# Storing one head's two gradients in pieces of 76, 48 and 4 rows from SyncE, and the last head's in halves: an attention-decode backward kernel on Trainium2

## The chip, the cores and the metric

The kernel runs on one core of one Trainium2 chip. The metric is device time in microseconds (us), as the median of several executions. Before the change it was 1286.64 us in three runs (1284.98 to 1289.45).

## The reference, cut to what matters

One query row per head attends to 8192 keys; wanted are the output and the gradients of q, k and v.

```python
B, H, Sq, Sk, D = 2, 32, 1, 8192, 128            # 64 heads, bf16

def _fwd_reference(q, k, v):
    scale = q.shape[-1] ** -0.5
    scores = jnp.einsum("bhqd,bhkd->bhqk", q, k) * scale
    p = _softmax(scores, axis=-1)
    return jnp.einsum("bhqk,bhkd->bhqd", p, v)

def reference(q, k, v, grad_out):
    _out, _vjp = jax.vjp(lambda *a: _fwd_reference(*a), q, k, v)   # shortened
    return (_out, *_vjp(grad_out))
```

For every head, k and v (2 MB each) are read and dk and dv (2 MB each) are written. dk and dv are outer products, so the arithmetic is small: 268.47 MB come in and 268.47 MB go out, and the memory traffic sets the time: 417 GB/s over the span before, with the DMA engines at nine tenths or more in 39 of the page's 40 slices.

## The kernel before

A head's k or v is one tile of 128 partitions with 64 rows of 128 numbers each. One partition of a 2 MB tile holds 16 KB. The gradient is written over the tile that held k or v, and stored from there; the load of a head six places later waits until that store has landed (116 such waits of SyncE's loads before, 1138.0 us in all).

```python
def by_rows(eng, dst, src, rows):                # a store cut along the partitions
    p = 0
    for m in rows:
        pin(eng.dma_start(out=dst[p : p + m], in_=src[p : p + m], max_dma_last_dim=NT * D))
        p += m

def outer(i, w, c, ends):                        # w = 1: v first, w = 0: k
    ...                                          # VectorE writes chunk c of the gradient
    if c + 1 in ends:
        at = ends.index(c + 1)
        b0, b1 = (ends[at - 1] if at else 0) * CH, (c + 1) * CH
        dst = (dv_v if w else dk_v)[i]
        if w == 0 and i in SPREAD:               # 7 of the 64 k stores: 126 + 2 rows
            by_rows(store_eng, dst, h.tile[w], (P - 2, 2))
        else:
            eng = load_eng if len(ends) > 1 else store_eng
            pin(eng.dma_start(out=dst[:, b0:b1, :], in_=h.tile[w][:, b0:b1, :]))

whole = [NCH]                                    # NCH = 4 chunks: one store
last = list(range(1, NCH + 1))                   # the last head: four quarters
...
for g in range(...):
    ...
    if x := within(O1):
        outer(x[0], 1, x[1], last if x[0] == BH - 1 else whole)
    if x := within(O0):
        outer(x[0], 0, x[1], last if x[0] == BH - 1 else whole)
```

`load_eng` is SyncE (queue q1 in the profile), `store_eng` is GpSimd (queue q0). So loads go through q1 and whole stores through q0, until the last head, 63, whose eight quarters go through q1. Both queues are served by the same 16 DMA engines: of their time the page gives q1 49.8% and q0 48.7%, and instructions (q8) 0.7%. After the loop, two small stores (o and dq, 16 KB each) leave from SyncE.

Of the kernel before, what the change touches and what calls it, by code (L numbers as in the profile page):

```python
# [20 lines left out]
SPREAD = range(5, 64, 9)  # L21
# [3 lines left out]
def kernel(  # L25
# [16 lines left out]
    BH = B * H  # L42
# [3 lines left out]
    NCH = NT // CH  # L46
# [3 lines left out]
    load_eng = nc.sync  # L50
# [32 lines left out]
    def by_rows(eng, dst, src, rows):  # L83
# [5 lines that stand above are left out]
# [299 lines left out]
    def outer(i, w, c, ends):  # L388

        h = heads[i]  # L390
        n0 = c * CH
        shape = [P, CH, D // 2, 2]
        pin(
            nc.vector.tensor_tensor(  # L394
                out=h.tile[w][:, n0 : n0 + CH, :].rearrange("p n (e t) -> p n e t", t=2),
                in0=h.qb[w][:]
                .rearrange("p (e t) -> p e t", t=2)
                .unsqueeze(1)
                .to_broadcast(shape),
                in1=h.pair[w][:, n0 : n0 + CH, :].unsqueeze(2).to_broadcast(shape),  # L400
                op=ALU.mult,
            )
        )
        if c + 1 in ends:
            at = ends.index(c + 1)
            b0, b1 = (ends[at - 1] if at else 0) * CH, (c + 1) * CH
            dst = (dv_v if w else dk_v)[i]
            if w == 0 and i in SPREAD:
                by_rows(store_eng, dst, h.tile[w], (P - 2, 2))
            else:  # L410
                eng = load_eng if len(ends) > 1 else store_eng
                pin(eng.dma_start(out=dst[:, b0:b1, :], in_=h.tile[w][:, b0:b1, :]))  # L412
# [3 lines left out]
    A0 = A1 + NCH  # L416
    O0 = A0 + 1
    whole = [NCH]
    last = list(range(1, NCH + 1))
    AHEAD = NTILE // 2  # L420

    prev = None
    for g in range(SL * BH + O0 + NCH + 4 - SL):
# [15 lines left out]
# [4 lines that stand above are left out]
        ev = None  # L443
        if g < SL * BH:
            i, r = divmod(g, SL)
# [74 lines left out]
```

## Time and profile before

| what | before |
|---|---|
| median of 3 runs | 1286.64 us |
| span of the profiled run, mean granted clock | 1286.9 us, 0.956 |
| traffic over the span | 417 GB/s |
| q1: loads, and head 63's stores | 272.70 MB, 49.8% of 16 engines |
| q0: whole stores | 264.25 MB, 48.7% of 16 engines |
| q8: instructions, 150 packets | 2.46 MB |

The page's list of DMA issues gives what, from which engine's queue, how often, KB each, and the median us from issue to landing. Two of its lines for the kernel before:

```profile
out_dram<-kvt POOLq DMA_DIRECT2D x119, 2048.0 KB, 66.9
out_dram<-kvt SPq DMA_DIRECT2D x8, 512.0 KB, 24.0
```

A whole store takes 67 us to land although its 8 rows per engine are only some 5 us of packets (8 x 0.61): it must stand in line behind other stores, which leave about every 10 us. At the end of the program such a line remains on each engine, and it isn't equally long on all of them: by the prediction's chains of packets the engines end their data between 1259.8 and 1284.7 us. The prediction below shows the lines of the end.

### The profile page before, as it was taken

To read this page: it belongs to the slowest core of one execution; us is meant where nothing else is said; L and a number is where in the kernel's file an instruction comes from. 1 tells how busy PE (TensorE), PEld (TensorE's weight loads), DVE (VectorE), ACT (ScalarE), POOL (GpSimd) and SP (SyncE) were. 2 spreads that over 40 slices of the span, in tenths; PEclk is the share of its full clock that TensorE was granted. 3 is DMA by queue.
4 is the path that set the end of the run, shared out by engine and by line. 5 is a ranking of instruction groups with operands and counts; after the bars stand their busy time and mean duration, and the time that the engine had idled before them with its cause. 6 is when DMAs were issued, how large, how long until landed. Compare 5 with 4: busy or idle time off the path is not lost.

```text
span 1286.9 us, 42575 instructions
## 1 busy us (share of the span) xinstructions
PE 1131.8 (88%) x19268; PEld 860.1 (67%) x19268; DVE 935.9 (73%) x2122; ACT 975.2 (76%) x641; POOL 75.1 (6%) x142
## 2 busy tenths in 40 slices
PE   6999999988899988989899988889898988988880
PEld 5777777766677666766666766667666666766650
DVE  2888888777687777767776876777767777777781
ACT  6888888877788777867777877778777777777750
POOL 0000000000000000000000000000000000000000
PEclk9999999999899999989899998999999999999985
DMA  9999999999999999999999999999999999999995
GB/s 388 424 425 427 427 427 427 426 427 428 428 426 427 428 427 426 416 429 427 427 427 429 427 427 427 427 424 424 426 427 428 426 427 424 427 428 428 424 392 216
DMA packets 39986, 539.68 MB, mean 419 GB/s; under 512 B 5116, under 2 KB 5116, under 8 KB 6396
## 3 DMA queue, kind: packets, MB, share of 16 engines
q1 hardware_dynamic: 20172, 272.70, 49.8%
q0 software_dynamic: 19632, 264.25, 48.7%
q8 instruction: 150, 2.46, 0.7%
q14 instruction: 32, 0.26, 0.0%
HBM read 268.47 MB, written 268.47 MB: 417 GB/s over the span
## 4 chain that ended last, share of the span: by engine, by line
DMA 38%; PE 26%; another core or an unknown queue 19%; DVE 10%; issue 4%; ACT 1%; SPq 1%; POOL 0%; POOLq 0%; DVEq 0%; ACTq 0%
DMA kvt<-in_v_dram 29%; PE tp L184 11%; PE acc L339 6%; DVE kvt L394 6%; DMA kvt<-in_k_dram 5%; DMA out_dram<-kvt 4%; PE dpw L195 3%; PE sw L195 3%; DVE sel L362 2%; ACT ev L186 1%; PE dpw L282 1%; SPq L98 1%; DVE sel L356 1%; DMA qd_nat<-in_q_dram 1%
## 5 line engine op out<-in xcount | busy, mean ns | idle before, releaser
L186 ACT COPY ev<-tp 128x2048 bf16<-128x2048 bf16 x512 | 954.4, 1865 | 266.1 <-PE tp L184 254.4
L184 PE MATMUL tp<-ident_bf,kvt 128*128 128x128 bf16 x8192 | 559.9, 223 | 91.6 <-DMA kvt<-in_v_dram 71.6
L394 DVE TENSOR_TENSOR kvt<-qb,pair 128x2048 bf16<-128x2048 bf16 x512 | 621.4, 1214 | 0.3
L184 PEld LDWEIGHTS <-kvt 128*128 128x128 bf16 x8192 | 490.5, 101 | 98.3 <-DMA kvt<-in_v_dram 75.1
L195 PEld LDWEIGHTS <-ev 128*128 128x128 bf16 x8192 | 243.1, 96 | 210.0 <-issue 152.5
L339 PE MATMUL acc<-kvt,dS_pad 128*64 128x512 bf16 x1024 | 169.2, 413 | 0.8 <-DVE dqT L379 0.8
L339 PE MATMUL acc<-kvt,E_pad 128*64 128x512 bf16 x1024 | 161.0, 395 | 0.0
L195 PE MATMUL dpw<-qdT,ev 128*128 128x1 bf16 x4096 | 140.8, 164 | 17.7 <-DVE qb L177 16.9
L362 DVE SCALAR_TENSOR_TENSOR sel<-acc,diag,sel 128x128 f32<-128x128 f32 x384 | 134.7, 351 | 13.6
L195 PE MATMUL sw<-qdT,ev 128*128 128x1 bf16 x4096 | 142.0, 164 | 1.2 <-ACT ev L186 1.2
L412 POOL DMA_DIRECT2D out_dram<-kvt x119 | 63.7, 536 | 1087.6 <-DVE kvt L394 922.1
L207 DVE TENSOR_REDUCE mp<-sw 128x1 f32<-128x64 f32 x64 | 14.4, 224 | 151.8 <-PE sw L195 151.8
L339 PEld LDWEIGHTS <-dS_pad 128*64 128x64 bf16 x1024 | 37.7, 111 | 24.7 <-issue 5.9
L247 DVE CAST E_pad<-E_f 128x64 bf16<-128x64 f32 x64 | 12.5, 195 | 55.4 <-ACT E_f L238 55.4
L339 PEld LDWEIGHTS <-E_pad 128*64 128x64 bf16 x1024 | 36.5, 109 | 21.4 <-issue 0.9
L376 PE MATMUL acc<-ones,sel 128*128 128x1 f32 x256 | 43.6, 239 | 6.2 <-DVE sel L362 6.2
L282 PE MATMUL dpw<-ld,ones 128*128 128x1 f32 x256 | 46.3, 250 | 0.1
L253 DVE CUSTOM_DVE_ANT_0 junk<-E_f,dpw 128x64 bf16<-128x64 f32 x64 | 14.1, 221 | 43.7 <-PE dpw L195 43.7
L376 PEld LDWEIGHTS acc<-ones,sel 128*128 128x128 f32 x256 | 39.3, 194 | 7.3 <-DVE sel L362 7.3
L356 DVE TENSOR_SCALAR sel<-acc,diag 128x128 f32<-128x128 f32 x128 | 44.1, 344 | 0.0
L177 DVE CAST qb<-dpw 128x128 bf16<-128x128 f32 x128 | 35.5, 277 | 6.2 <-PE dpw L168 6.2
L282 PEld LDWEIGHTS dpw<-ld,ones 128*128 128x128 f32 x256 | 38.2, 189 | 0.5 <-DVE ld L253 0.5
(44 smaller groups left out, 313.2 us busy)
## 6 DMA issues: line engine op xcount, KB each, us to landing
out_dram<-kvt POOLq DMA_DIRECT2D x119, 2048.0 KB, 66.9
kvt<-in_v_dram SPq DMA_DIRECT2D x64, 2048.0 KB, 20.9
kvt<-in_k_dram SPq DMA_DIRECT2D x63, 2048.0 KB, 20.9
out_dram<-kvt POOLq DMA_DIRECT2D x7, 2016.0 KB, 70.3
out_dram<-kvt SPq DMA_DIRECT2D x8, 512.0 KB, 24.0
kvt<-in_k_dram SPq DMA_DIRECT2D x2, 512.0 KB, 4.7
kvt<-in_k_dram SPq DMA_DIRECT2D x1, 1024.0 KB, 7.3
out_dram<-kvt POOLq DMA_DIRECT2D x7, 32.0 KB, 69.7
```

The source lines that it names most:

```text
L177: pin(nc.vector.tensor_copy(out=h.qb[w][:], in_=h.qbp))
L184: pin(nc.tensor.transpose(tp[:, t, :], src[:, c * CH + t, :], ident_bf[:]))
L186: pin(nc.scalar.copy(out=ev[:], in_=tp[:]))
L195: nc.tensor.matmul(dst[:, c * CH + t : c * CH + t + 1], lhsT=ev[:, t, :], rhs=qdT[:, w, i : i + 1], start=True, stop=True,)
L207: pin(nc.vector.reduce_max(out=h.mp[:], in_=h.s, axis=AX.X))
L282: nc.tensor.matmul(out, lhsT=ones[:].to_broadcast([P, P]), rhs=col, start=True, stop=True)
L339: nc.tensor.matmul(h.acc[w][g : g + CW, :], lhsT=wts[:, n0 : n0 + CW], rhs=rows[:, n0 : n0 + QT, :].rearrange("p n d -> p (n d)"), start=( ...
L356: nc.vector.tensor_scalar(out=h.sel[:], in0=block, scalar1=diag[:, 0:1], scalar2=None, op0=ALU.mult)
L362: nc.vector.scalar_tensor_tensor(out=h.sel[:], in0=block, scalar=diag[:, b : b + 1], in1=h.sel[:], op0=ALU.mult, op1=ALU.add,)
L376: nc.tensor.matmul(h.acc[w][:, 0:1], lhsT=h.sel[:], rhs=ones[:], start=True, stop=True)
L394: nc.vector.tensor_tensor(out=h.tile[w][:, n0 : n0 + CH, :].rearrange("p n (e t) -> p n e t", t=2), in0=h.qb[w][:] .rearrange("p (e t) -> ...
L412: pin(eng.dma_start(out=dst[:, b0:b1, :], in_=h.tile[w][:, b0:b1, :]))
```

## The change

The intent is to balance the 16 DMA engines at the end. Head 62's two stores are taken from GpSimd's queue and cut so that four engines carry 23 of the 128 rows each and the other twelve 3 each. The four are called engines 0 to 3 here. SyncE gets six larger pieces, so head 63's eight quarters become four halves.

```diff
-            if w == 0 and i in SPREAD:
+            if i == BH - 2:
+                by_rows(load_eng, dst, h.tile[w], (76, 48, 4))
+            elif w == 0 and i in SPREAD:
                 by_rows(store_eng, dst, h.tile[w], (P - 2, 2))
...
-    last = list(range(1, NCH + 1))
+    last = [NCH // 2, NCH]
```

## The prediction

> **What bounds the kernel now.** I began with the busy slices of the page, because the change touches only stores of the last two heads.
>
> ```profile
> PE   6999999988899988989899988889898988988880
> DMA  9999999999999999999999999999999999999995
> GB/s 388 424 425 427 427 427 427 426 427 428 428 426 427 428 427 426 416 429 427 427 427 429 427 427 427 427 424 424 426 427 428 426 427 424 427 428 428 424 392 216
> ```
>
> Each digit is a fortieth of the span (32 us). DMA is at 9 everywhere but in the last slice, where the rate halves to 216 GB/s: the body is bound by data movement, and the only loose time is the end. So I asked for stretches of the end (columns: us, busy us and instructions of PE, PEld, DVE, ACT, POOL, the granted clock, DMA share, GB/s).
>
> ```profile
> 1180.00:1230.00 50.00, 43.08 (x755) 32.79 (x752) 36.04 (x84) 37.45 (x27) 3.55 (x6) 1.00 1.01 424
> ...
> 1240.00:1246.00 6.00, 4.70 (x56) 2.75 (x56) 5.34 (x14) 1.86 (x1) 0.53 (x1) 0.84 0.86 339
> 1246.00:1258.00 12.00, 6.03 (x27) 2.44 (x23) 11.43 (x20) 0.00 (x0) 0.00 (x0) 0.50 1.01 420
> 1258.00:1262.00 4.00, 0.63 (x3) 0.36 (x3) 0.57 (x3) 0.00 (x0) 0.00 (x0) 0.50 0.84 349
> 1262.00:1274.00 12.00, 0.00 (x0) 0.00 (x0) 0.00 (x0) 0.00 (x0) 0.00 (x0) 0.50 0.57 241
> 1274.00:1281.00 7.00, 0.00 (x0) 0.00 (x0) 0.00 (x0) 0.00 (x0) 0.00 (x0) 0.50 0.41 169
> 1281.00:1287.00 6.00, 0.00 (x0) 0.00 (x0) 0.00 (x0) 0.00 (x0) 0.00 (x0) 0.50 0.05 19
> ```
>
> From 1262 us on nothing computes, yet stores run for 23 us more with a DMA share of 0.57, then 0.41: some of the 16 DMA engines have run dry while others still have a queue. The end is the end of the slowest single DMA engine, and the mean of the share says nothing of it.
>
> The timeline of the two issuing queues gives the arrivals:
>
> ```profile
> 1233.65 0.53 POOL L412 DMA_DIRECT2D out_dram<-kvt  x1 [8.19 <-DVE kvt L394]
> 1243.38 0.53 POOL L412 DMA_DIRECT2D out_dram<-kvt  x1 [9.19 <-DVE ld L253]
> ```
>
> ```profile
> 1245.80 11.98 SPq L412 DMA_DIRECT2D out_dram<-kvt  x8
> 1259.23 4.90 SPq L489 DMA_DIRECT2D out_dram<-nat  x2
> ```
>
> The first two are the stores of head 62 (v, then k), the third the eight quarters of head 63.
>
> No view splits packets by DMA engine, so I did it from the trace's packet records. An engine runs one packet at a time, and its next packet starts 3 to 4 ns before the recorded end of the one before; chaining back from the end, with every engine held to its known share of each SyncE store, gives 16 chains. Last data packet of each:
> - seven late chains: 1279.9, 1280.0, 1280.2, 1280.9, 1280.9, 1281.5 and 1284.7 us;
> - two at 1272.8 and 1273.7 us;
> - seven early: 1259.8 (three), 1260.2, 1260.7, 1261.3 and 1263.7 us.
>
> The span ends 2.05 us after the last packet of all (1284.85, then 1286.9). Why are there two groups? The 150 instruction-fetch packets (q8, 16 KB, about 1 us each) fall in a strict round of eight chains, some 19 us of work on each. The seven late ones are seven of these; the eighth is one of the two chains that the 126+2-row stores relieve (14 packets of 8 KB there instead of 126).
>
> [...] SyncE's queue holds 2258 completion packets, 141 x 16 and 2, and the 2 are the 58-row load's. [...] that load and the 6-row load at the start give a set of six chains [...], and only one of the eight instruction-fetch chains is among them, a relieved one. That places engines 0 to 3 in the early group. [...] in the trace a late engine alternates one by one (16 KB of q0, 4 KB of q1)[...].
>
> **The change part by part.** A 16 KB row costs 0.607 us from start to start (0.611 recorded, 4 ns overlap); the two 8 KB halves of a split row cost 2 x 0.305.
> 1. Before, each store of head 62 puts 8 rows on every engine. After, engines 0 to 3 get 19 + 3 + 1 = 23, the others 3.
> 2. Late engines: 2 stores x 5 rows fewer = 10 x 0.607 = **-6.1 us**. They have no idle time in the end stage, so they finish that much earlier: 1284.85 becomes 1278.8, the other six about 1274 to 1275.5.
> 3. Engines 0 to 3: 2 x 15 = 30 rows more, 18.2 us. Part of it fills holes: early chains idle 2.3 to 5.1 us around 1240 to 1245, waiting for head 62's k. Counting work from 1228 us: the five earliest candidates have 26 to 35 packets of 16 KB on q0 left (16 of them head 62) and 16 equivalents of head 63. After: 26 - 16 + 16 + 46 = 72, to 35 - 16 + 16 + 46 = 81, times 0.607 = 44 to 49 us: done at **1272 to 1277 us**. If the 1263.7 chain (39 packets) is one of them, 1280.
> 4. Head 63 in halves: the same bytes, 32 packets of 8 KB for 64 of 4 KB on each engine: 9.76 against 9.92 us, -0.16 us. The first half starts when the second quarter did (1247.8 instead of 1245.8); an early engine may idle, a late one has its backlog.
> 5. GpSimd issues two stores less (0.53 us each), off the path.
>
> Sum: the last packet at 1278.7 instead of 1284.85, about **6 us** less. Nothing before 1233 us is touched.
>
> **The rivals.**
> - *Engines 0 to 3 become the bound.* If the numbering were otherwise and they were late ones, 1281 + 18.2 + 2 = 1301 us (+1.1%). Against it: the set of six above, and that the change aims at them. In a milder form, an early engine with more backlog ends at 1280 and eats 1 to 2 us of the gain.
> - *A wait for a semaphore.* SyncE's issues rotate over eight completion semaphores, so issue n waits for n-8 to land. After the change the third half of head 63 waits for the 76-row piece of v. On engines 0 to 3 this is 38 packets of 8 KB, alternating with some 13 of 16 KB: 13 x 0.916 + 25 x 0.305 = 19.5 us after about 1234.5, so 1254, just when the half is ready (1253.9). The last small store waits for the 76-row piece of k: about 1268. Neither is the end, unless landings come 10 us later than this; then up to 1290.
> - *SyncE stalls on deep queues.* 2 x 46 packets can be queued on engines 0 to 3. Before, SyncE had up to 72 (8 stores of 8 packets and a completion) queued on a late engine without stopping; its issues took 0.8 to 1.7 us instead of 0.34. A stall of a few us is hidden behind the late engines' backlog; a long one would cost up to 8 us, 1289.
> - *Hidden anyway*, about 1286: against it, nothing but stores runs in the last 23 us.
>
> **Range and chances.** 1286.64 - 6 = 1280.6; I take 1281.0 as engines 0 to 3 may be the last in some runs. The three runs of before spread over 4.5 us, and the late chains lie within 5 us of each other, so 1277.5 to 1285.5. A gain over 2% would need 26 us, more than the whole idle tail holds: 1%. A loss over 2% needs the wrong engines and a stall: 1%.
>
> **What would show it.** In the profile after: SyncE issues six stores of head 62 at about 1234 and 1243; the DMA share stays near 1 until 1258 without the dip to 0.86 at 1240, and is well above 0.57 between 1262 and 1274; by engine, four chains with 92 packets of 8 KB for head 62 where the others have 12, ending at 1272 to 1280, and the late ones 6 us earlier. The prediction is wrong if one of those four chains ends last by more than 2 us, if SyncE stands in an issue or a wait for head 62's landings past 1265, or if the late chains do not move by 6 us.

## The result, and the profile after

| | before | after |
|---|---|---|
| median of the rounds together (4 runs each) | 1288.05 us | 1307.70 us |
| lowest to highest | 1284.98 to 1296.05 | 1305.86 to 1308.69 |
| span, clock of the profiled run | 1286.9 us, 0.956 | 1306.9 us, 0.952 |

The ratio is 1.0141, with a 95% interval from 1.0093 to 1.0190: slower by some 18 us, where 6 us less were predicted. A ratio here is the mean time of one kernel's fast runs over that of the other's of the same rounds, so it isn't quite the ratio of the medians. The loss is under 2%, but far outside the range of 1277.5 to 1285.5.

The page's busy slices of the kernel after (tenths of DMA busy time, and the rate, in fortieths of the span):

```profile
DMA  9999999999999999999999999999999999999982
GB/s 387 425 427 429 425 427 427 428 427 426 428 427 428 427 429 415 425 428 427 428 426 423 426 426 428 427 426 425 426 428 430 426 424 425 429 427 427 403 283 95
```

Up to slice 37 nothing has moved. The last two slices fell from 392 and 216 GB/s to 283 and 95: all the loss lies in the end, where the change is. The stretches of the end, with the columns of the prediction (us, busy us of PE, PEld, DVE, ACT, POOL, granted clock, DMA share, GB/s), of the kernel after:

```profile
1240.00:1246.00 6.00, 5.17 (x84) 3.54 (x82) 4.61 (x14) 3.52 (x4) 0.00 (x0) 1.00 0.84 289
1246.00:1258.00 12.00, 7.07 (x29) 3.04 (x29) 11.78 (x20) 0.00 (x0) 0.00 (x0) 0.50 0.81 277
1258.00:1262.00 4.00, 0.90 (x3) 0.63 (x3) 2.25 (x8) 0.00 (x0) 0.00 (x0) 0.50 0.81 240
1262.00:1274.00 12.00, 0.00 (x0) 0.00 (x0) 0.00 (x0) 0.00 (x0) 0.00 (x0) 0.50 0.91 304
1274.00:1281.00 7.00, 0.00 (x0) 0.00 (x0) 0.00 (x0) 0.00 (x0) 0.00 (x0) 0.50 0.72 225
1281.00:1287.00 6.00, 0.00 (x0) 0.00 (x0) 0.00 (x0) 0.00 (x0) 0.00 (x0) 0.50 0.28 94
1287.00:1307.00 20.00, 0.00 (x0) 0.00 (x0) 0.00 (x0) 0.00 (x0) 0.00 (x0) 0.50 0.13 53
```

Three things are to be read here. First, from 1246 to 1258 us the share is 0.81 where it was 1.01, and the rate 277 GB/s where it was 420. The rate fell more than the share: per unit of share it was 420 / 1.01 = 416 GB/s and is 277 / 0.81 = 342. So engines stand idle, and those at work move less. Second, at 1262 to 1274 the share is indeed higher than before (0.91 against 0.57), as predicted. Third, from 1287 to 1307 us a share of 0.13 is two engines of 16 on average: very few engines end the program.

The timeline of SyncE's issues after (start, us taken, queue, line, what, how many):

```profile
1235.55 23.27 SPq L87 DMA_DIRECT2D out_dram<-kvt  x6
1258.94 17.12 SPq L414 DMA_DIRECT2D out_dram<-kvt  x4
1276.15 17.27 SPq L491 DMA_DIRECT2D out_dram<-nat  x2
```

SyncE was held up for almost the whole tail: the four halves of head 63 left over 17 us from 1258.94 on, and the last small store only at 1292.95. Taken one by one from the trace, the 48-row piece of k took 9.70 us to issue, the 4-row piece after it 3.58 us, and three of the four halves 3.4 to 3.9 us each; in the kernel before the quarters took 0.34 to 1.7 us. SyncE's waits after (engine, line, what it waited for: us in total, times, longest):

```profile
SPq L491 <- DMA out_dram<-kvt: 9.7, 1, 9.7
SPq L414 <- DMA out_dram<-kvt: 5.2, 2, 2.9
```

The third half (line 414) waited until 1269.26 us for the 76-row piece of v to land, and the last small store (line 491) until 1292.89 for that of k. So the two waits that the prediction named do happen, each for the issue eight places before (the ninth for the first, the twelfth for the fourth), but 15 and 25 us later than it reckoned.

Landings, engine by engine, come from completion packets (4 bytes; q1's 2258 before are 16 for each of 141 transfers and 2 for the 58-row load, and SyncE's wait for v's 76-row piece ended at 1269.26 us, with the last of that piece's four at 1269.3). Of the 76-row pieces only four engines have one: v's landed at 1254.8, 1255.5, 1263.4 and 1269.3 us, k's at 1274.0, 1281.4, 1289.7 and 1292.9. The fourth half landed on twelve engines at 1279.4 to 1282.7, and on the last four at 1288.5, 1293.6, 1302.1 and 1305.4. **Engines 0 to 3 became the end of the program**, up to 25 us later than the 1280 that step 3 reckoned for them at worst. (That the four latest are the four with the 76-row pieces is read from the times: each landed its half 12 to 15 us after one of the pieces of k, in the same order, and all others were done by 1282.7.)

Did these four ever wait for SyncE? Their piece of k had been issued by 1245.46 us, before the first of them was through with v's, and the fourth half by 1276.05. Paired in order, the three that ended last landed the fourth half 12.2 to 12.5 us after the 76-row piece of k. Between the two stand 40 packets of 8 KB, so 0.31 us each: no pause. The late halves didn't leave these three without work.

### The profile page after: what moved, and what is told of

It is laid out like the page before. It is cut to its first block, busy times and chain, and to the rows that moved or that the text cites.

```text
span 1306.9 us, 42572 instructions
## 1 busy us (share of the span) xinstructions
PE 1128.2 (86%) x19268; PEld 857.8 (66%) x19268; DVE 935.8 (72%) x2122; ACT 975.1 (75%) x641; POOL 74.0 (6%) x140
## 3 DMA queue, kind: packets, MB, share of 16 engines
q1 hardware_dynamic: 20156, 276.90, 50.2%
## 4 chain that ended last, share of the span: by engine, by line
DMA 37%; another core or an unknown queue 24%; PE 18%; DVE 8%; issue 7%; ACT 1%; SPq 1%; POOL 0%; POOLq 0%; DVEq 0%; ACTq 0%
DMA kvt<-in_v_dram 15%; DMA kvt<-in_k_dram 13%; PE tp L184 8%; DMA out_dram<-kvt 7%; DVE kvt L394 5%; PE acc L339 4%; PE dpw L195 2%; PE sw L195 2%; DVE sel L362 1%; ACT ev L186 1%; SPq L98 1%; PE dpw L282 1%; DMA qd_nat<-in_q_dram 1%; DVE sel L356 0%
## 5 line engine op out<-in xcount | busy, mean ns | idle before, releaser
L247 DVE CAST E_pad<-E_f 128x64 bf16<-128x64 f32 x64 | 12.5, 196 | 54.8 <-ACT E_f L238 54.8
```

## The experiments

The prediction left three candidates for the loss, and one more showed itself in the packets:

- *The wrong engines.* One of engines 0 to 3 wasn't early at all, so that 30 more rows put it last. Working with bytes alone, this gives a definite end.
- *SyncE held up.* Head 63's halves come late because SyncE stands in issues and waits.
- *Slow packets.* A row stored in small groups of partitions may cost more than a row in a whole store. The durations of the 8 KB packets of q1 after 1233 us point to it: in the kernel after, 26% of the 1024 packets took 350 ns or more, 16% of them about double (580 to 660 ns), where the median is 309 ns.
- *The halves*, or SyncE as the issuer: something in the change other than the cut by rows.

Each text states what was expected of its run by the theories held at that time; where it says no more than "theory 1", that is the theory of slow packets. For the runs that follow, this table sums up what was measured; "before" is the median of the kernel before, the packet columns are for q1's 8 KB packets after 1233 us, and the last column is the end of the last data packet. These are 1024 packets, of heads 62 and 63; where head 63 leaves from GpSimd they are the 512 of head 62 alone, and with halves alone the 512 of head 63.

| run | median, us | before, us | ratio [95%] | mean packet, ns | 350 ns and more | last data, us |
|---|---|---|---|---|---|---|
| after | 1307.70 | 1288.05 | 1.0141 [1.0093, 1.0190] | 409 | 26% | 1305.06 |
| whole rows, SyncE | 1286.37 | 1289.13 | 0.9970 [0.9935, 1.0005] | 321 | 3% | 1284.63 |
| the same, again | 1285.04 | 1288.29 | 0.9976 [0.9962, 0.9990] | 319 | 3% | |
| halves alone | 1288.56 | 1288.01 | 0.9999 [0.9964, 1.0033] | 316 | 1% | |
| 64 + 64 rows | 1294.76 | 1288.90 | 1.0044 [1.0017, 1.0071] | 427 | 28% | 1293.15 |
| 8 x 16 rows | 1297.37 | 1289.13 | 1.0059 [1.0030, 1.0088] | 492 | 26% | 1293.06 |
| 8 x 16, spread in HBM | 1296.45 | 1288.01 | 1.0067 [1.0036, 1.0097] | 474 | 26% | 1291.7 |
| v only | 1293.53 | 1288.90 | 1.0034 [1.0013, 1.0056] | 367 | 16% | 1289.71 |
| three engines, v only | 1293.66 | 1288.29 | 1.0042 [1.0028, 1.0055] | 369 | 16% | 1289.38 |
| head 63 from GpSimd | 1300.52 | 1288.90 | 1.0089 [1.0068, 1.0110] | 420 | 34% | 1296.56 |
| cut in the middle, head 36 | 1293.44 | 1288.90 | 1.0038 [0.9997, 1.0079] | | | |

Unless a diff says otherwise, it is against the kernel after.

### Which engine is which: markers, before and after

The trace doesn't name the engine of a packet. Eight small loads of 13, 12, 8, 5, 4, 3, 2 and 1 rows (256 bytes each) were added near 1231 us. With them q1 holds 96 packets more (20252 against 20156, the kernel after with and without markers): 48 of data and 48 completion packets, one of each for every row. Engine n, for n up to 4, is here the name of the chain that holds a packet of the load of n + 1 rows but none of the load of n: engine 3 holds one of the load of 4 and none of the load of 3. That these engines 0 to 3 are the four of the 76-row pieces was the assumption; no record shows it. In both kernels:

```diff
             load(i + AHEAD, 1)
+            if i + AHEAD == BH - 1:
+                for m in (13, 12, 8, 5, 4, 3, 2, 1):
+                    t = work.tile([16, D], BF16, tag=f"mark{m}", name="mark")
+                    pin(load_eng.dma_start(out=t[:m, :], in_=k_v[0][:m, m, :]))
```

The kernel before, with markers:

> The kernel before, with eight tiny marker loads (13, 12, 8, 5, 4, 3, 2 and 1 rows of 256 B) behind the last load, [...]. Time as before, 1284 to 1291 us. If my reading of the numbering was right, engines 0 to 3 end their data at 1259 to 1264 us and the late ones are 6 to 12 with one more. If it was wrong, at least one of engines 0 to 3 ends past 1272 us.

Measured, one run, state unknown: 1287.77 us, so the markers cost nothing to speak of. Chained packet by packet, the ends of the engines are:

```text
engine                     last data, us   16 KB packets of q0 left after 1236 us
0                          1260.5          13
1                          1261.8          25
2                          1262.25         23
3                          1268.7          34
4 (relieved by 126 + 2)    1273.8          not counted
5 (relieved by 126 + 2)    1260.7          not counted
seven of 6 to 15           1279.9-1284.25  48
```

Engines 0, 1 and 2 are early, and **engine 3 isn't** (at 1268.7 it lies between the two outcomes that the expectation named). It also carries the 8 KB instruction packets (q14) at 1043.4, 1111.3, 1191.0 and 1256.9 us. In the unmarked trace of before, the chain with those packets (1041.8, 1111.9, 1191.5, 1256.4) is the one that ended at 1273.7 us, one of the "two at 1272.8 and 1273.7" which the prediction put between its groups. If it is one of the four, it would end, with 30 rows more, at 1273.7 + 30 x 0.607 = 1291.9 us by bytes alone, so the span at 1294. That explains 7 us of the loss (1291.9 against 1284.85), not 18. It may be less: in the marked run engine 3 ended 5 us earlier, and the same sum from there gives 1268.7 + 18.2 = 1286.9, a loss of 2 us.

The kernel after, with markers:

> The changed kernel with the same markers; time as after, 1303 to 1311 us. Theory 1 [...]: engines 0 to 3 had no more queued than in the marked kernel before, but their 8 KB packets of head 62 take 400 to 600 ns instead of 309[...]. Rival (wrong engines): two of engines 0 to 3 have 15 or more 16 KB packets of the other queue left at 1236 us than the early engines, and those two end last, whatever their rows.

Measured, one run, state unknown: 1302.97 us. **Inconclusive.** Four chains end their data late, at 1299.6, 1295.8, 1292.7 and 1286.9 us, but packets of several engines ran in step and the marks couldn't be attributed with certainty. So which of engines 0 to 3 was last isn't known. The 48-row piece of k took 15.2 us to issue here, against 9.7 in the unmarked run.

### Whole rows from SyncE

Everything of the change stays but the cut:

```diff
             if i == BH - 2:
-                by_rows(load_eng, dst, h.tile[w], (76, 48, 4))
+                pin(load_eng.dma_start(out=dst, in_=h.tile[w], max_dma_last_dim=NT * D))
```

> Head 62 on SyncE, but each store whole (128 rows, 8 per engine); halves as in the change. Theory 1 (the uneven rows do the harm): 1283 to 1291 us, as before. Rival (moving head 62 to SyncE's queue does it, by long issues that hold up head 63): 1298 us or more.

Measured: 1286.37 us, ratio 0.9970. The loss is gone, so it comes from the cut by rows. SyncE's issues, and two of the stretches, of this run:

```profile
1233.62 10.58 SPq L409 DMA_DIRECT2D out_dram<-kvt  x2
1248.50 8.81 SPq L414 DMA_DIRECT2D out_dram<-kvt  x4
1259.93 1.87 SPq L491 DMA_DIRECT2D out_dram<-nat  x2
```

```profile
1246.00:1258.00 12.00, 5.39 (x27) 2.11 (x23) 11.74 (x21) 0.00 (x0) 0.00 (x0) 0.56 1.00 417
1262.00:1274.00 12.00, 0.00 (x0) 0.00 (x0) 0.00 (x0) 0.00 (x0) 0.00 (x0) 0.50 0.56 239
```

A line of the timeline covers the time between its issues too: the two whole stores themselves took 0.41 and 0.39 us and the halves 0.33 to 0.34 each; the rest is time between them. (In the kernel after, where the waits were read, line 87 waited 20.3 and 4.9 us for VectorE.) The engines are as full as before from 1246 to 1258 and move 417 GB/s at a share of 1.00. The unequal end (0.56 at 1262 to 1274) is back.

### Whole rows again

The same kernel once more with five rounds, because a gain of a quarter of a per cent needs them.

> The kernel with head 62 whole on SyncE and head 63 in halves once more, with five rounds, as the one version so far not slower than before (ratio 0.997): 1283 to 1289 us, ratio 0.995 to 1.000.

Measured: 1285.04 us against 1288.29, ratio 0.9976 [0.9962, 0.9990]. This is the best version, faster than both kernels, though by only 0.24%. Why it is faster than before wasn't tested: halves alone give nothing (next run), so it presumably lies in head 62's stores going through SyncE.

### Halves alone

The kernel before with one line changed:

```diff
-    last = list(range(1, NCH + 1))
+    last = [NCH // 2, NCH]
```

> The second part of the change alone: head 63's stores in halves, head 62 as before. Nothing of the late engines' work changes but -0.16 us of packets, so 1284 to 1291 us, the same as before within 3 us. If halves were at fault for a part of the loss, 1291 us or more.

Measured: ratio 0.9999 [0.9964, 1.0033]. Halves neither gain nor lose. This agrees with step 4 of the prediction (-0.16 us), as far as 0.3% can.

### 64 + 64 rows

```diff
-                by_rows(load_eng, dst, h.tile[w], (76, 48, 4))
+                by_rows(load_eng, dst, h.tile[w], (64, 64))
```

q1 holds 20172 packets here against 20140 with whole rows: 32 more, so the two pieces added left 16 completion packets each. So, evenly shared, each of the 16 engines gets 4 rows of each piece and 8 rows of a store, as in a whole store. By bytes this run equals the one with whole rows.

> Head 62 on SyncE in two stores of 64 rows [...]. Theory 1 [...] 8 KB packets of head 62 average 450 ns or more and the time is 2 to 10 us above that of whole stores. Rival [...]: packets 309 to 345 ns, time within 3 us of the whole stores.

Measured: 1294.76 us, ratio 1.0044, with a mean packet of 427 ns. Bytes per engine are the same as with whole rows, and 28% of the packets are slow. One stretch of this run:

```profile
1246.00:1258.00 12.00, 6.77 (x29) 2.73 (x28) 11.75 (x21) 0.00 (x0) 0.00 (x0) 0.50 0.99 279
```

At 0.99 the engines are as busy as with whole rows (1.00), yet they move 279 GB/s instead of 417, a third less. A busy share says that packets are open, not that bytes flow.

By the packet, an undisturbed 8 KB packet takes 309 ns, which is 8192 / 309 = 26.5 GB/s for one engine; the slow packets of the kernel after lie about 580 to 660 ns, which is 12.4 to 14.1 GB/s, half of it. With whole rows 3% of the packets took 350 ns or more, here 28%. What makes them slow isn't shown.

### 8 x 16 rows

```diff
-                by_rows(load_eng, dst, h.tile[w], (76, 48, 4))
+                by_rows(load_eng, dst, h.tile[w], (16,) * 8)
```

Again every engine gets 8 rows of each store, but now one of each piece (q1 holds 20364 packets, 224 more than with whole rows: 16 completion packets for each of the 14 pieces added). The 16 rows of a piece lie on 16 neighbouring partitions.

> Head 62 on SyncE in eight stores of 16 neighbouring rows each: every engine still gets 8 rows of each store[...]. Theory 1 [...]: 8 KB packets of these stores take 600 ns or more on average against 309, and the kernel is 5 to 20 us slower than with whole stores. Rival (only the number of rows per engine counts): packets stay near 309 to 340 ns and the time is that of the whole stores within 3 us.

Measured: 1297.37 us, ratio 1.0059, mean packet 492 ns; a tenth of the packets took over 1.0 us and one in a hundred over 2.3 us. Narrower pieces have slower packets: 321 ns with 128 rows, 427 with 64, 492 with 16. These means include head 63. The packets that began before SyncE issued head 63's first half are head 62's alone, and there the order is plainer: 343 ns with whole rows, 523 with 64, 664 with 16, so the 600 ns or more that was expected did come (in the kernel after it is 456). Part of this run's time is another cost, which its issues show:

```profile
1233.14 37.15 SPq L87 DMA_DIRECT2D out_dram<-kvt  x16
1270.39 10.95 SPq L414 DMA_DIRECT2D out_dram<-kvt  x4
1281.76 2.69 SPq L491 DMA_DIRECT2D out_dram<-nat  x2
```

The first piece took 0.36 us to issue and the other 15 took 1.2 to 4.4 us each, and the last half left at 1279.81 us, so that head 63 itself came late. The packet durations are free of this, the total time isn't.

### 8 x 16 rows, spread in HBM

The slow packets could also come from the writing side, 16 neighbouring rows of one region of HBM (the main memory) at a time. Here the 16 partitions stay neighbours, but their rows go to places eight rows apart. The result is wrong: dk and dv of head 62 are permuted (relative error of dk 0.19).

```diff
-                by_rows(load_eng, dst, h.tile[w], (76, 48, 4))
+                for j in range(8):
+                    pin(load_eng.dma_start(out=dst[j::8], in_=h.tile[w][16 * j : 16 * j + 16], max_dma_last_dim=NT * D))
```

> As the stores of 16 neighbouring rows, but each writes them to rows of the output that lie 8 apart (128 KB instead of 16 KB), so dk and dv of head 62 come out permuted, wrong on purpose. Theory 1 [...]: as before this edit, 8 KB packets average 450 ns or more (492 with neighbouring rows on both sides) and 1293 to 1299 us. Rival (neighbouring rows of HBM are the shared thing): packets 309 to 345 ns, 1283 to 1290 us.

Measured: 1296.45 us, mean packet 474 ns, against 492 with neighbouring rows; of head 62 alone, counted as above, 663 against 664. Spreading the writes doesn't help, so neighbouring rows in HBM aren't what slows the packets. That points to the reading side. It doesn't prove it: the reverse test, spread partitions with neighbouring rows, was not run, nor any other spacing in HBM.

### v only

```diff
-                by_rows(load_eng, dst, h.tile[w], (76, 48, 4))
+                by_rows(load_eng, dst, h.tile[w], (76, 48, 4) if w else (P,))
```

> Uneven rows for v of head 62 alone, k whole on SyncE: engines 0 to 3 get 15 rows more instead of 30. By bytes alone (my prediction's sum): late engines 3.05 us earlier, about 1283 us. Theory 1 (packets slowed [...], 0.12 us on each of the 92 - 46 = 46 packets less than in the change, and 9 us of bytes less): 1288 to 1295 us, between before and the change.

Measured: 1293.53 us, ratio 1.0034. By bytes alone engine 3, if it is one of the four, would end its data at 1273.7 + 15 x 0.607 = 1282.8 and the late engines at about 1281.7, so the span near 1285. The profiled span was 1291.5 us with its last data at 1289.71, 7 us later. The mean packet (367 ns) lies between that of whole rows and that of the full change. Half of the cut gives back part of the loss, but doesn't turn it into a gain. Late issues have little part in this: the four halves left SyncE at 1248.82 to 1257.30 us, each 0.3 us after its counterpart with whole rows, and only the last took long to issue (3.33 us).

### Three engines, v only

If engine 3 was the only trouble, a cut that spares it must gain. Pieces of 93, 32 and 3 rows are to run on 3, 16 and 3 engines: engines 0 to 2 then get 31 + 2 + 1 = 34 rows, the others 2. That is the estimate, from the 2 engines of the 58-row load and the 4, 16 and 4 of the 76-, 48- and 4-row pieces; on which engines these pieces ran isn't shown.

```diff
-                by_rows(load_eng, dst, h.tile[w], (76, 48, 4))
+                by_rows(load_eng, dst, h.tile[w], (93, 32, 3) if w else (P,))
```

> v of head 62 alone in stores of 93, 32 and 3 rows: [...] By bytes: engines 0 to 2 (last data at 1260 to 1264 us before) get 26 x 0.607 = 15.8 us more and end by 1280, late engines end 6 x 0.607 = 3.6 us earlier, so about 1283 us. If engine 3's own backlog made the loss of the change, this one is clear of it. Theory 1 [...]: packets of head 62's v on engines 0 to 2 well over 309 ns, and 1288 us or more.

Measured: 1293.66 us, ratio 1.0042 [1.0028, 1.0055]. By bytes, with that estimate, the slowest is a late engine at 1284.25 - 6 x 0.607 = 1280.6, and engine 2 ends at 1262.25 + 26 x 0.607 = 1278.0, so the span at 1283. It was 1291.1, with the last data at 1289.38. Packets: 369 ns in the mean. SyncE's issues of this run:

```profile
1233.93 10.07 SPq L87 DMA_DIRECT2D out_dram<-kvt  x4
1248.29 9.43 SPq L414 DMA_DIRECT2D out_dram<-kvt  x4
1273.22 2.01 SPq L491 DMA_DIRECT2D out_dram<-nat  x2
```

The halves left at 1248.29 to 1256.76 us, each 0.2 us before its counterpart with whole rows, in 0.33 to 0.95 us; only the two small stores were late. So SyncE's hold-up has no part in this loss, and if the pieces ran as estimated, engine 3's backlog has none. **Even a cut meant to spare engine 3 loses**: 1293.66 us against 1288.29.

### Head 63 from GpSimd

The halves of the last head leave through the other queue, so that SyncE can't hold them up:

```diff
-                eng = load_eng if len(ends) > 1 else store_eng
+                eng = store_eng
```

> The change, with head 63's halves issued by GpSimd instead of SyncE, so that SyncE's long issues (up to 9.7 us) hold up nothing but the two last small stores. Theory 1: the end is that of engines 0 to 3, which had work all along, so 1298 to 1310 us. Rival (the long issues make the loss): 1279 to 1290 us.

Measured: 1300.52 us, ratio 1.0089, against 1.0141 of the change. SyncE's issues and one stretch of this run:

```profile
1235.49 26.54 SPq L87 DMA_DIRECT2D out_dram<-kvt  x6
1262.13 7.03 SPq L491 DMA_DIRECT2D out_dram<-nat  x2
```

```profile
1287.00:1295.00 8.00, 0.00 (x0) 0.00 (x0) 0.00 (x0) 0.00 (x0) 0.00 (x0) 0.50 0.12 50
```

SyncE stood in head 62's pieces as long as before (2.4 to 9.9 us for the slow ones), so the hold-up is a matter of those pieces, not of the halves. With head 63 in the other queue the time falls by 0.0052 x 1288 = 7 us; 11 us remain. The two were run each against its own runs of the kernel before; the ratios' difference is hardly larger than their uncertainty, but the times don't overlap (1299.92 to 1301.33 against 1305.86 to 1308.69). The 11 us are head 62's alone: head 63's halves had landed on every engine by 1285.7 us, and the last piece of k landed on its four engines at 1286.5, 1287.4, 1294.8 and 1296.9. How the other queue saves the 7 us isn't shown; as the landings of the kernel after told, it isn't by feeding engines that stood without work. The end is again two engines (a share of 0.12), and the packets are as slow as ever (420 ns).

### The cut in the middle of the run

If unequal stores cost only at the end, where nothing can follow them, the same cut in the middle should relieve the late engines for the rest of the run. So the kernel before got the cut for head 36's k, from GpSimd. The line before the pieces and the small dummy load after them are meant to choose the engines; that the pieces fell on the intended ones wasn't checked.

```diff
             dst = (dv_v if w else dk_v)[i]
-            if w == 0 and i in SPREAD:
+            if w == 0 and i == 36:
+                pin(store_eng.inc_swdge_sem([], [], mode="reset_dge_cursor"))
+                by_rows(store_eng, dst, h.tile[w], (76, 48, 4))
+                t = work.tile([16, D], BF16, tag="turn", name="turn")
+                pin(store_eng.dma_start(out=t[:14, :], in_=k_v[0][:14, 0, :]))
+            elif w == 0 and i in SPREAD:
                 by_rows(store_eng, dst, h.tile[w], (P - 2, 2))
```

(This diff is against the kernel before.)

> The kernel before, with the same 76, 48 and 4 rows for one store in mid-run (k of head 36) on GpSimd's queue[...]. Theory 1 [...]: 3 us of relief for the late engines arrive, 1282 to 1287 us. Rival (uneven rows always cost what they gave at the end): 1292 us or more.

Measured: 1293.44 us (1291.01 to 1299.48), ratio 1.0038 [0.9997, 1.0079]. A miss for the hope of a gain; the interval just includes no change. Stretches after the cut, first of the kernel before, then of this run:

```profile
780.00:800.00 20.00, 18.09 (x300) 13.58 (x297) 14.22 (x33) 15.08 (x10) 1.06 (x2) 0.91 1.01 428
800.00:820.00 20.00, 18.09 (x298) 13.57 (x297) 14.21 (x33) 14.90 (x10) 1.06 (x2) 0.91 1.00 425
```

```profile
780.00:800.00 20.00, 18.18 (x301) 13.73 (x297) 14.29 (x34) 15.03 (x10) 0.53 (x1) 0.91 0.98 397
800.00:820.00 20.00, 12.12 (x214) 9.12 (x213) 11.63 (x26) 11.51 (x8) 2.65 (x5) 0.85 1.00 406
```

Some 55 us after the cut (723.9 us) the rate sags to 397 and 406 GB/s, and PE loses 6 us of 20. No store is issued from 783.6 to 800.5 us. A load must wait for an earlier store of its tile to land (116 waits, 1138.0 us, in the kernel before), and a store has landed when its slowest engine has finished (v's 76-row piece in the kernel after: 1254.8 to 1269.3 us on its four engines, the wait for it until 1269.26); a store with most of its rows on four engines lands later, which would explain the pause. This is argued: the late landing wasn't separated from the packets, which were slower too: 369 ns for q0's 8 KB packets from 750 to 800 us. Those of the 126 + 2 stores, which are cut by rows as well, took 309 to 321 ns in mid-run: a cut that leaves nearly all partitions in one piece is not slow.

## Why the prediction was wrong

**The shape of the end** was right: the end is that of the slowest single DMA engine, there are early and late ones, nothing else runs from 1262 us on, and the rest of the run was not touched. The rows per engine (23 and 3) and the number of engines per piece were right: q1's completion packets went from 2258 to 2242, that is 2258 - 8 x 16 + 2 x (4 + 16 + 4) + 4 x 16.

All three signs of being wrong that the prediction listed appeared, and the share that was to stay near 1 until 1258 us fell to 0.81.

**Step 2**, the late engines 6 us earlier, is only partly borne out. The twelve other engines landed their last half at 1279.4 to 1282.7 us: the slowest of them is 2 us earlier than 1284.85, not 6. They had to wait for the fourth half, which SyncE issued only at 1272.67 us and took 3.4 us over: nine of them landed it within 0.4 us of each other, at 1279.4 to 1279.8.

**The step that failed first** is the sentence "That places engines 0 to 3 in the early group". It was drawn from a set of six chains, which the author took to hold engines 0 to 3, and a set can't tell its members apart. Of the four that the markers name, three are early; engine 3 was the chain of 1273.7 us. The stated exception, "If the 1263.7 chain (39 packets) is one of them, 1280", was too mild: the chain of 1273.7 is one of those that the markers name. Markers, which cost 48 small packets, told these chains apart; that the 76-row pieces ran on these four stays the assumption.

**The step that failed most widely** is step 3's "times 0.607". The price of a row was taken from whole stores. In the change the mean 8 KB packet took 409 ns (456 where it is head 62's alone) instead of the 305 counted, and q0's 16 KB packets beside them 691 ns, against 625 with whole rows: the neighbours pay too. The runs with 64 + 64 and 8 x 16 rows show it with the bytes per engine unchanged, and the two runs with v alone show what it costs with SyncE on time. Why packets of narrow pieces are slow isn't shown: the durations rise from 343 through 523 to 664 ns as the pieces narrow from 128 through 64 to 16 rows, and spreading the rows in HBM leaves 663, but no run shows the cause.

**The rivals** were named and set too low. "SyncE stalls on deep queues" was given "up to 8 us, 1289" because the late engines' backlog would hide it; the stalls came (up to 9.70 us), and the fourth half left at 1272.67 us against 1256.98 with whole rows. But they set the end only of the twelve other engines; the three that ended last had SyncE's packets waiting all along, by their landings. Sending the halves through the other queue saved 7 us all the same, in a way that stays open. "A wait for a semaphore" was placed at 1254 and 1268 us; two of the four engines did land v's piece at 1254.8 and 1255.5, but the wait is for the slowest, 1269.3, and for k 1292.9. "Engines 0 to 3 become the bound" was put at 1301 us and came true at 1307.7. The three were weighed apart, though one feeds the other: more rows on an engine and slower packets give later landings, and the waits for these give later issues (v's piece landed at 1269.3 us, the third half waited until 1269.26, and the fourth left at 1272.67).

**The sum**, an estimate from the runs. In the profiled runs the last data came at 1284.7 us before and at 1305.06 after, 20 us later. Bytes alone explain 2 to 7 of these (30 rows on engine 3, if it is one of the four, from its end in the marked or the unmarked run). The main part of the rest is the price of the rows: all packets after 1233 us took 717 us together on the 16 engines, against 599 us with whole rows, for nearly the same bytes (15.3 and 15.1 MB). With v alone, half of the cut and SyncE's halves on time, this price shows by itself: the last data came 7 and 9 us later than bytes say (1289.71 against 1282.8, and 1289.38 against 1280.6). The 7 us that head 63 from GpSimd saved overlap with this, since its packets took 692 us; the parts can't be added up.

**What stays open:** which engines the 76-row pieces ran on, and which of them ended last; what makes the packets of narrow pieces slow; why an issue behind a first piece takes 1.1 to 15.2 us when that first piece takes 0.3 to 0.7 and a whole store 0.4 (it isn't the depth of the queues on four engines alone, since 8 x 16 rows, with no engine favoured, took 1.2 to 4.4 us per piece; nor the size of the piece, since halves of all 128 rows behind such pieces took up to 4.6 us); how head 63 from the other queue saves 7 us; whether the cut in the middle costs anything (0.9997 to 1.0079), and by what; and why whole stores from SyncE gain 0.24%.

## What to carry to other kernels

Before you move rows from one DMA engine to another, look at two things: the backlog that each engine already has, and how narrow the group of partitions is that a piece covers. A cut that balances bytes can lose more through slow packets than it balances (343 ns with whole stores, 523 with 64 rows, 664 with 16). Find out which engine is which with small marker transfers rather than by argument, and read the busy share together with GB/s, because a share of 1.00 stood for 417 GB/s in one kernel and 0.99 for 279 in the next. At the end of a program, prefer whole 128-partition stores (1285 us here, against 1293 to 1308 for the cuts by rows that were tried), and try the other queue for what must leave last when many small pieces are being issued in one (7 us here).

## Two more measured things

- How long an issue from SyncE stands when stores are cut: 0.39 to 0.41 us for a whole 2 MB store, 1.2 to 4.4 us for a 16-row piece (the first 0.36), 1.95 to 15.2 us for the 48-row piece behind one of 76 rows.
- Instruction fetch loaded the DMA engines unequally: by the prediction's chaining, 150 packets of 16 KB, about 1 us each (986 ns in the mean), fell on only eight of the 16 engines in a fixed round, some 19 us on each, and 8 KB ones came to engine 3 every 66 to 80 us towards the end. That this made the engines unequal in the first place is the guess; no run changed it.
